# Linear attention beside an MLP: a tile of its own for one head group's rows, sums issued at separate ticks, and a wider pad

## The chip, the cores and the metric

The kernel runs on one core of one Trainium2 chip. The time is device microseconds (us) of that core, the median of several executions. Engines are named as in the profile: PE (TensorE products), PEld (its weight loads), DVE (VectorE), ACT (ScalarE), POOL (GpSimd), SP (SyncE, which issues the DMAs here). `L70` is line 70 of the kernel before.

## The reference

All float32, S = 2048 tokens, D = 640, H = 32 heads of Dh = 20, F = 1728. The result is the input plus an attention branch plus an MLP branch, both on the layer norm of the input:

```
xn  = layernorm(x)
q, k, v = split(xn @ wqkv)                      # per head, 20 wide
pq, pk  = q @ w_phi[h], k @ w_phi[h]
phi     = concat(softmax(p), softmax(-p))       # 40 features per head
o   = phi_q (phi_k^T v) / (phi_q (phi_k^T 1) + 1e-6)
out = x + o @ wo + gelu(layernorm(xn) @ w1 + b1) @ w2 + b2
```

There is no mask: `phi_k^T v` and `phi_k^T 1` are sums over all tokens, so no token's attention output can be made before the last token's `k` and `v`.

## The kernel before

**Numbers.** Each float32 operand is kept as a high and a low part of TensorE's rounded 32-bit type. One product of two operands is three matmuls, high by high, high by low and low by high, which `mm3` issues on lines 70, 71 and 72. Nearly all have 128x128 weights (the stationary operand) and 512 moving columns. In the profile's notation `bank<-y,w` the first name is the moving operand, the second the stationary.

**Stages.** The tokens are four blocks of 512, the hidden units of the MLP 14 chunks of 128 in seven pairs `g`.
- To 215 us: layer norm, transposes, and the MLP for blocks 0 and 1 (`passes`).
- 215 to 446 us: the `q`, `k`, `v` products for 16 tiles of 128 tokens. L895 holds them; each tile takes, over five rows of 128 features, `q` and `k` columns from `wkh` and `wkl`, and the third column group and `v` from tiles named `w`. Their stationary operand is `y`, the normalised tokens. The softmax features of `q` go to DRAM (`e_dram`); those of `k` are multiplied with `v` at once (L965).
- 446 to 478 us: the sums over `k` and `v` become the stationary tiles `kvs`, one for each of 11 head groups.
- 478 to 660 us: the MLP for blocks 2 and 3, with the attention output of all four blocks beside it. For pairs 1 to 5 the method `cross` does w1's part with fewer products, a 2x2 scheme with sums of w1's quarters as weights and sums of the tokens (`tf`) as moving operand; `sums` makes those of w1.
- 660 to 737 us: the product with `wo`, added to the rest and stored.

**What runs beside.** After each triple of products the MLP calls `mlp.tick()`. A tick runs the steps that have come due and moves the generator `beside` one step on. `after(n, step)` puts a step in the list, due in `n` ticks. In the stage from 478 us the order of work on ACT, DVE and POOL is the order in which the program issues it; on each of these engines an instruction that waits holds all behind it. SP's order is chosen by the scheduler.

**Attention's output.** `Attention(b)` takes block `b` through the head groups in the order 10, 0, 1, ..., 9. Groups 0 to 9 have three heads each, group 10 the last two. For a group, `load` brings 128 rows of features from DRAM into `e`, `first` splits them into a high part (ACT, L1195) and a low part (POOL, L1196). Some ticks later `second` issues the products with `kvs` (L1202, L1203) into a bank of PSUM; ACT copies half of the bank's rows into `ts` (L1212), and two ticks later DVE adds the other half (L1216), which frees the bank. For groups 0 to 9 the sum goes to `ob`. For group 10 it goes back into the same rows of `ts`, from which two DMAs send 40 rows of outputs to `o_dram` (L1218) and 2 rows of denominators to `d_dram` (L1219). `ts` is one tile with one buffer.

**Quotients.** Once a block's groups are done, `quotients` gathers the denominators through DRAM into `dt`, takes the reciprocal on DVE (L1235), sends it back, and loads it into five places of `rx` (L1240 to L1245). DVE spreads it over the rows of each head (`stream_shuffle`, L1251) and POOL multiplies the outputs (L1253). This runs beside the next block's groups. L336 and L455 are DVE's own additions and low parts for the MLP; L443, L449 and L452 are ACT's copy, gelu and high part.

**The sums.** `sums(g)` makes one sum and three differences of w1's quarters on POOL in four instructions of 128x256 (L381); ACT and POOL or DVE then split them into the weights of pair `g`. For pairs 2 to 5 it is called by the third of the steps that `gathered` hands to `cross`; for pair 1 before the loop.

**Where tiles lie.** Pools stand on a left and a right side of SBUF. The first pool on the left, `consts`, ends with a tile `pad` that nothing uses (L83). All left tiles of the products (`y`, `m`, `w`, `v`, the accumulators of blocks 0 and 1) begin at a byte of their partition that is 32 modulo 256; the right side's (`wkh`, `wkl`, `tf`, `kvs`, `e`, `ph`) at 224 modulo 256.

Of the kernel before, what the change touches and what calls it, by code (L numbers as in the profile page):

```python
# [8 lines left out]
F32 = mybir.dt.float32  # L9
F32R = mybir.dt.float32r  # L10
AF = mybir.ActivationFunctionType
ALU = mybir.AluOpType
# [3 lines left out]
P = 128  # L16
# [35 lines left out]
def tile_kernel(ctx: ExitStack, tc: tile.TileContext, x, xT, wkT, wqT, wv, wphi, wo, w1, b1, w2, b2,  # L52
                ident, mmask, emask, vsel, out):
    nc = tc.nc
# [20 lines left out]
    cp = ctx.enter_context(tc.tile_pool(name="consts", bufs=1))  # L75
# [4 lines left out]
    mv = cp.tile([P, 16, 2], F32, name="mv")  # L80
    ry = cp.tile([P, 16], F32, name="ry")
    rs_all = cp.tile([P, 16], F32, name="rs_all")
    cp.tile([P, 8], F32, name="pad")  # L83
    nc.vector.memset(ones1, 1.0)
    nc.scalar.activation(rs_all[0:1, 0:1], ones1[:, 0:1], AF.Sqrt)

# [18 lines left out]
    class Banks:  # L105

        def __init__(self, *ids):
            self.ids, self.n = ids, 0
# [15 lines left out]
    def load_x(ts, xp, tag="xb"):  # L124
        xbs = []
        for t in ts:
            xb = xp.tile([P, D], F32, name=tag)
            nc.sync.dma_start(xb, x[t * P:(t + 1) * P, :])
            xbs.append(xb)
        return xbs  # L130
# [83 lines left out]
    class Mlp:  # L214
# [11 lines left out]

        def after(self, ticks, step):

            self.due.append((self.ticks + ticks, len(self.due) and self.due[-1][1] + 1, step))
            self.due.sort(key=lambda d: d[:2])  # L230

        def fetch(self, c, pool=None):

# [94 lines left out]
        def second(self, g, b, w, hid):  # L328

            for m in range(KC):  # L330
                pw = self.po()
                ms = slice(m * P, (m + 1) * P)
                for j, (hh, hl) in enumerate(hid):
                    mm3(pw, w[:, 2 * j, ms], w[:, 2 * j + 1, ms], hh, hl, j == 0, j == 1)
                    self.tick()
                nc.vector.tensor_tensor(acc[b][:, m, :], pw, acc[b][:, m, :], op=ALU.add)  # L336
                yield

        def fetch_pair(self, g, second):

            r1 = rp.tile([P, D], F32, name="r1")
            r2 = rp.tile([P, D], F32, name="r2")
            self.raw[g, second] = r1, r2
            for c, r in ((2 * g, r1), (2 * g + 1, r2)):
                n = min(P, F - c * P)
                if second:
                    for o in range(0, P, n):
                        nc.sync.dma_start(r[o:o + n, :], w2[c * P:c * P + n, :])
                else:
                    nc.sync.dma_start(r.rearrange("p (c f) -> p c f", f=P)[:, :, 0:n], w1[c, :, :, 0:n])  # L350

        def take_pair(self, g, second, slot):

            w = wp.tile([P, 4, D], F32R, name=f"w{slot}")

            def part(j, r):
                hi, lo = w[:, 2 * j], w[:, 2 * j + 1]
                if 0 < g < 6:
                    return self.split(hi, lo, r)
                if 2 * g + j < 13:  # L360
                    split(hi, lo, r, eng=nc.gpsimd)
                elif second:
                    nc.scalar.activation(hi, r, AF.Copy)
                    nc.vector.memset(f(lo[64:128, :]), 0.0)
                    nc.vector.tensor_tensor(lo[0:64, :], r[0:64, :], f(hi[0:64, :]), op=ALU.subtract)
                else:
                    hi, lo, r = (z.rearrange("p (c f) -> p c f", f=P) for z in (hi, lo, r))
                    split(hi[:, :, 0:64], hi[:, :, 64:128], r[:, :, 0:64])
                    nc.vector.memset(f(lo[:, :, 64:128]), 0.0)
                    nc.vector.tensor_copy(lo[:, :, 0:64], f(hi[:, :, 0:64]))  # L370

            return w, [lambda j=j, r=r: part(j, r) for j, r in enumerate(self.raw.pop((g, second)))]

        def sums(self, g):

            raw = [r.rearrange("p (c f) -> p c f", f=P) for r in self.raw[g, False]]
            (a11, a12), (a21, a22) = ((r[:, 0:4:2, :], r[:, 1:4:2, :]) for r in raw)
            s = rp.tile([P, 3, 2, P], F32, name="s")
            for out, x0, x1, op in ((s[:, 0], a21, a22, ALU.add), (a21, a11, a21, ALU.subtract),
                                    (s[:, 1], s[:, 0], a11, ALU.subtract), (s[:, 2], a12, s[:, 1], ALU.subtract)):  # L380
                nc.gpsimd.tensor_tensor(out, x0, x1, op=op)  # L381
            self.raw[g, "s"] = s

        def split(self, hi, lo, src, eng=nc.gpsimd):
# [126 lines left out]
    mlp = Mlp((0, 1, 2, 3), ((0, 2), (1, 3)))  # L511
# [8 lines left out]
    x0 = load_x(range(2), xp)  # L520
    nc.sync.dma_start(idt, ident)
    wc, parts, dmas = {}, {}, {}
# [23 lines left out]
    x1 = load_x(range(4, 8), xp)  # L546
# [16 lines left out]
    def step(gen, n):  # L563
        for _ in range(n):
            next(gen, None)
# [169 lines left out]
    def prep():  # L735
# [60 lines left out]
        for q in range(3):  # L796
            tiles = [(c, b) for c in range(2 * q, min(2 * q + 2, KC)) for b in range(2, 4)]
            for n, at in enumerate(tiles):
                for after, step in ((-6, load), (0, centred), (3, scaled), (5, hi), (7, lo)):
                    events.append((base + 5 * n + after, len(events), step, at))  # L800
            base += 5 * len(tiles) + 5
            if q < 2:
                for n, i in enumerate((0, 2, 1, 3)):
                    for after, step in ((0, combine), (3, lambda q, i: hi(*combined(q, i)[0])), (5, combined_lo)):
                        events.append((base + 4 * n + after, len(events), step, (q, i)))
                base += 19
# [65 lines left out]
    a = ExitStack()  # L872
# [133 lines left out]
    for t, i in [(t, i) for t in range(14) for i in range(4)] + TAIL:  # L1006
# [35 lines left out]
        if (t, i) == (11, 0):  # L1042
            mlp = Mlp((0, 3, 2, 1), ((1, 2), (0, 3)))
            mlp.ph = ptile
            mlp.fetch_pair(0, False)
        if (t, i) == (12, 3):
            with tc.issue_after(evac):
                w1t, parts = mlp.take_pair(0, False, 0)
# [3 lines left out]
        if (t, i) == (15, 3):  # L1052
            w2t, late = mlp.take_pair(0, True, 3)
# [97 lines left out]
    class Attention:  # L1151

        def __init__(self, b, bank):
            self.b, self.n, self.bank = b, 0, bank
            self.ob = acc01.tile([P, KC, 512], F32, name=f"acc{b % 2}")
            self.ts = ep.tile([P, 512], F32, name="ts")
            self.es = {}

        def load(self, g):
# [39 lines left out]
        def second(self, g, ph, pl):  # L1199

            pn = self.bank()
            nc.tensor.matmul(pn, kvs[:, g, :], ph, start=True, stop=False)  # L1202
            nc.tensor.matmul(pn, kvs[:, g, :], pl, start=False, stop=True)  # L1203
            c, h = divmod(g, 2)
            den = d_dram[self.b][0]
            if g < 10:
                a, z = slice(64 * h, 64 * h + VR), slice(64 - 64 * h, 64 - 64 * h + VR)
                t, o = self.ts[a, :], self.ob[a, c, :]
            else:
                a, z = slice(0, 42), slice(64, 106)  # L1210
                t = o = self.ts[a, :]
            nc.scalar.activation(t, pn[z, :], AF.Copy)  # L1212


            def whole():
                nc.vector.tensor_tensor(o, pn[a, :], t, op=ALU.add)  # L1216
                if g == 10:
                    nc.sync.dma_start(o_dram[self.b], o[0:40])  # L1218
                    nc.sync.dma_start(den[30:32, :], o[40:42])  # L1219

            mlp.after(2, whole)
# [78 lines left out]
    ep = rx = None  # L1300
# [42 lines left out]
    ep = ctx.enter_context(tc.tile_pool(name="eB", bufs=1, side="right", reuse_waits="tile"))  # L1343
# [4 lines left out]
    def gathered(g):  # L1348

        w2t, parts = mlp.take_pair(g, True, 0 if g % 2 else 3)  # L1350

        def second():
            parts[1]()
            mlp.after(2, lambda: mlp.fetch_pair(g + 1, False))

        return w2t, [parts[0], second, lambda: g < 5 and mlp.sums(g + 1)]

    for g in range(1, 6):
        w2t, later = gathered(g)
        hid, more = mlp.cross(g, (2, 3), before, later)  # L1360
        if g < 5:
            parts = mlp.splits(g + 1)
        else:
            w1t, parts = mlp.take_pair(6, False, 1)
        for m, _ in enumerate(mlp.second(g, 2, w2t, hid[0])):
            next(more, None)
            if m < len(parts):
                parts[m]()
            if m == 3:
                mlp.fetch_pair(g + 1, True)  # L1370
        before = mlp.second(g, 3, w2t, hid[1])
# [5 lines left out]
    w2t, parts = mlp.take_pair(6, True, 3)  # L1377
# [14 lines left out]
    step = 0  # L1392
# [79 lines left out]
```

## Time and profile before

| | us |
|---|---|
| runs before: median (lowest, highest) | 735.54 (735.34, 735.95) |
| the profiled execution | 739.13 |
| its span, first to last instruction | 737.3 |
| PE busy, 0 to 215 | 215.00 of 215 |
| PE busy, 215 to 446 | 230.67 of 231 |
| PE busy, 446 to 478 | 31.50 of 32 |
| PE busy, 478 to 660 | 168.06 of 182 |
| PE busy, 660 to 737 | 73.92 of 77 |
| mean granted TensorE clock, 478 to 660 | 0.97 |
| mean granted TensorE clock elsewhere | 1.00 |

The rows by stage come from one view that gives each engine's busy time in stretches of the span. Matmuls are pipelined, so a duration in the trace (some 390 ns for 512 columns) is longer than the step from the start of one to the start of the next, and a busy PE can still be made faster by a shorter step. PE is hardly ever idle outside the fourth and the last stretch. Of the fourth, where attention's output runs beside the MLP, it is idle 13.9 us. In the views below, the brackets behind an instruction hold the idle time of its engine just before it, and which engine or DMA ended it.

### The profile page before, as it was taken

The numbers are of one execution on the slowest core, as the hardware profiler recorded it, in microseconds if no ns is written. First come the engines' busy times: TensorE is split into PE (matmuls) and PEld (weight loads), VectorE is DVE, ScalarE is ACT, GpSimd is POOL, SyncE is SP. The second block draws the span as 40 slices with busy tenths as digits, with TensorE's granted clock in tenths as the row PEclk, the third lists the DMA queues.
The fourth block names the chain that finished last, engine by engine and source line by source line (L and its number), as shares of the span: only waits on it lengthen the run. The fifth ranks groups of instructions, "written<-read, shape, count | busy, mean of one in ns | idle before, by whom it ended". The sixth has DMA issues, their size and how long they took to land.

```text
span 737.3 us, 9741 instructions
## 1 busy us (share of the span) xinstructions
PE 713.9 (97%) x3381; PEld 594.6 (81%) x3381; DVE 518.3 (70%) x820; ACT 342.2 (46%) x563; POOL 423.0 (57%) x360
## 2 busy tenths in 40 slices
PE   9989999999999999999999999999989986999998
PEld 7878888878888888888888888888767864878886
DVE  7777756978646887888977896486786853875531
ACT  6534643434235554454445456476665743560110
POOL 3511313675256987887879787585696972641200
PEclk9999999999999999999999999999999998999999
DMA  9813633585531246156005148834354467254122
GB/s 331 281 49 113 195 102 108 170 258 170 196 135 47 70 171 168 55 187 170 1 1 140 43 158 305 239 120 126 114 178 137 135 211 275 66 190 139 72 85 73
DMA packets 65767, 106.56 MB, mean 145 GB/s; under 512 B 7462, under 2 KB 31814, under 8 KB 63838
## 3 DMA queue, kind: packets, MB, share of 16 engines
q1 hardware_dynamic: 65414, 105.93, 44.6%
q8 instruction: 26, 0.43, 0.2%
q14 instruction: 23, 0.19, 0.1%
q10 hardware_dynamic: 304, 0.01, 0.0%
HBM read 71.37 MB, written 34.55 MB: 144 GB/s over the span
## 4 chain that ended last, share of the span: by engine, by line
PE 82%; DVE 5%; POOL 4%; DMA 4%; issue 2%; ACT 2%; SPq 0%; POOLq 0%; ACTq 0%; DVEq 0%
PE bank L895 27%; PE bank L70 15%; PE bank L71 15%; PE bank L72 15%; PE bank L965 2%; PE bank L693 2%; DMA d<-ts 1%; POOL e L1196 1%; POOL w L387 1%; PE bank L1203 1%; PE bank L1202 1%; DMA t<-t 1%; POOL acc L1253 1%; DVE m L455 1%; DMA r<-sr 1%
## 5 line engine op out<-in xcount | busy, mean ns | idle before, releaser
L895 PE MATMUL bank<-wkh,y 128*128 128x512 f32 (+1 forms) x480 | 141.1, 367 | 0.0
L70 PE MATMUL bank<-y,w 128*128 128x512 f32 (+1 forms) x294 | 115.0, 391 | 0.8 <-ACT m L280 0.8
L70 PE MATMUL bank<-m,w 128*128 128x512 f32 x260 | 104.0, 400 | 11.4 <-DVE acc L336 7.1
L72 PE MATMUL bank<-y,w 128*128 128x512 f32 (+1 forms) x294 | 114.3, 389 | 0.0
L71 PE MATMUL bank<-y,w 128*128 128x512 f32 (+1 forms) x294 | 114.2, 389 | 0.0
L64 POOL TENSOR_TENSOR w<-r,w 128x640 fp32r<-128x640 f32 x32 | 53.5, 1684 | 98.8 <-ACT w L61 68.0
L71 PE MATMUL bank<-m,w 128*128 128x512 f32 x260 | 102.2, 393 | 0.0
L72 PE MATMUL bank<-m,w 128*128 128x512 f32 x260 | 102.1, 393 | 0.0
L895 PEld LDWEIGHTS bank<-wkh,y 128*128 128x128 f32 x480 | 87.4, 188 | 14.5
L895 PE MATMUL bank<-wkl,y 128*128 128x512 f32 (+1 forms) x240 | 87.8, 366 | 0.0
L70 PEld LDWEIGHTS bank<-m,w 128*128 128x128 f32 x260 | 49.5, 190 | 24.7 <-DVE acc L336 7.5
L70 PEld LDWEIGHTS bank<-y,w 128*128 128x128 f32 x294 | 55.5, 189 | 12.4 <-ACT m L280 1.0
L72 PEld LDWEIGHTS bank<-y,w 128*128 128x128 f32 x294 | 55.5, 189 | 11.6
L71 PEld LDWEIGHTS bank<-y,w 128*128 128x128 f32 x294 | 55.6, 189 | 11.2
L931 ACT ACTIVATE m<-m,rs_all 128x1280 f32<-128x1280 f32 x32 | 43.7, 1365 | 40.0 <-POOL m L930 39.9
L933 DVE TENSOR_REDUCE sm<-m 128x64 f32<-128x1280 f32 x32 | 47.4, 1480 | 15.4 <-ACT m L931 15.3
L72 PEld LDWEIGHTS bank<-m,w 128*128 128x128 f32 x260 | 49.3, 190 | 10.7
L895 PE MATMUL bank<-w,y 128*128 128x512 f32 x240 | 57.5, 391 | 0.0
L71 PEld LDWEIGHTS bank<-m,w 128*128 128x128 f32 x260 | 49.4, 190 | 10.0
L930 POOL TENSOR_TENSOR m<-m,mx 128x640 f32<-128x640 f32 (+2 forms) x48 | 44.4, 938 | 19.5 <-DVE mx L919 19.5
L325 DVE TENSOR_TENSOR acc<-bank,acc 128x512 f32<-128x512 f32 x70 | 47.0, 683 | 12.0 <-PE bank L321 6.2
L1212 ACT ACTIVATE ts<-bank 64x512 f32<-64x512 f32 (+1 forms) x44 | 26.1, 593 | 56.3 <-PE bank L1203 35.6
(181 smaller groups left out, 1472.1 us busy)
## 6 DMA issues: line engine op xcount, KB each, us to landing
r<-in_w SPq DMA_DIRECT2D x52, 320.0 KB
e<-e SPq DMA_DIRECT2D x40, 256.0 KB
e<-acc SPq DMA_DIRECT2D x52, 160.0 KB
acc<-in_xT SPq DMA_DIRECT2D x4, 1280.0 KB
t<-t SPq DMA_DIRECT2D x8, 512.0 KB
tf<-t SPq DMA_DIRECT2D x2, 1536.0 KB
xb<-in_x SPq DMA_DIRECT2D x8, 320.0 KB
xq<-in_xT SPq DMA_DIRECT2D x10, 256.0 KB
```

The source lines that it names most:

```text
L64: eng.tensor_tensor(lo, src, f(hi), op=ALU.subtract)
L70: nc.tensor.matmul(ps, lh, rh, start=first, stop=False, **kw)
L71: nc.tensor.matmul(ps, lh, rl, start=False, stop=False, **kw)
L72: nc.tensor.matmul(ps, ll, rh, start=False, stop=last, **kw)
L325: nc.vector.tensor_tensor(acc[b][:, m, :], pw, acc[b][:, m, :], op=ALU.add)
L693: nc.tensor.matmul(ps[:, u * nh * DF:(u + 1) * nh * DF], raw[:nh * DH, u * P:(u + 1) * P], wpt[:nh * DH, g, :nh, 1:], start=True, stop=True)
L895: nc.tensor.matmul(ps, lh[:, kc, c], rh[:, kc], start=n == 0, stop=n == 3 * KC - 1)
L930: subs[n, t] = nc.gpsimd.tensor_tensor(ep[:, s], a, b, op=ALU.subtract)
L931: exps[n, t] = nc.scalar.activation(e, e, AF.Exp, scale=rs_all[:, t:t + 1])
L933: nc.vector.tensor_reduce(sm, e.rearrange("p s (h f) -> p (s h) f", f=DH), axis=AX, op=ALU.add)
L965: nc.tensor.matmul(kvp[g // 2][:, (g % 2) * 240:(g % 2) * 240 + 240].rearrange("p (s f) -> p s f", s=4), v[:, g * VS:(g + 1) * VS], ft[:, ...
L1212: nc.scalar.activation(t, pn[z, :], AF.Copy)
```

## The change

Three edits. The tile `pad` gets 56 columns of float32 instead of 8, so that every left tile moves by 192 bytes, from 32 to 224 modulo 256. `sums` takes a number `apart`: its four instructions are issued that many ticks from one another, with the first at once; pairs 2 to 5 pass 1. For this `after` runs a step at once when its ticks are 0. And group 10's rows get a tile `t10` of 42 rows, into which ACT copies, DVE adds and from which the two DMAs read.

```diff
-    cp.tile([P, 8], F32, name="pad")
+    cp.tile([P, 56], F32, name="pad")
...
         def after(self, ticks, step):
 
-            self.due.append((self.ticks + ticks, len(self.due) and self.due[-1][1] + 1, step))
-            self.due.sort(key=lambda d: d[:2])
+            if ticks:
+                self.due.append((self.ticks + ticks, len(self.due) and self.due[-1][1] + 1, step))
+                self.due.sort(key=lambda d: d[:2])
+            else:
+                step()
...
-        def sums(self, g):
+        def sums(self, g, apart=0):
...
-            for out, x0, x1, op in ((s[:, 0], a21, a22, ALU.add), (a21, a11, a21, ALU.subtract),
-                                    (s[:, 1], s[:, 0], a11, ALU.subtract), (s[:, 2], a12, s[:, 1], ALU.subtract)):
-                nc.gpsimd.tensor_tensor(out, x0, x1, op=op)
+            for i, (out, x0, x1, op) in enumerate(((s[:, 0], a21, a22, ALU.add), (a21, a11, a21, ALU.subtract),
+                                                   (s[:, 1], s[:, 0], a11, ALU.subtract), (s[:, 2], a12, s[:, 1], ALU.subtract))):
+                self.after(i * apart, lambda out=out, x0=x0, x1=x1, op=op: nc.gpsimd.tensor_tensor(out, x0, x1, op=op))
...
             self.ts = ep.tile([P, 512], F32, name="ts")
+            self.t10 = ep.tile([42, 512], F32, name="t10")
...
-                t = o = self.ts[a, :]
+                t = o = self.t10[a, :]
...
-        return w2t, [parts[0], second, lambda: g < 5 and mlp.sums(g + 1)]
+        return w2t, [parts[0], second, lambda: g < 5 and mlp.sums(g + 1, 1)]
```

The lines behind the edits move by 3 to 4: L381 becomes L384, L1196 becomes L1200, L1212 becomes L1216. PE, ACT and DVE keep their order; SP's differs by a place in two pairs of neighbours (a weight load beside an `e` load). On POOL the sums are pulled apart. The next rows are POOL's in the fourth stage, at the sums for pair 4; `s` and the tiles `r` belong to the sums, L1196 is the low part of attention's next head group, L1253 the multiplication by the quotients, L387 the first split of a sum. Before:

```order
L1253 TENSOR_TENSOR acc_4392<-acc_4392,rx 128x512
L381 TENSOR_TENSOR s<-r_5013 128x256
L381 TENSOR_TENSOR r_5013<-r_5012,r_5013 128x2x128
L381 TENSOR_TENSOR s<-s,r_5012 128x256
L381 TENSOR_TENSOR s<-r_5012,s 128x256
L1196 TENSOR_TENSOR e<-e,ph 128x512
L1253 TENSOR_TENSOR acc_4392<-acc_4392,rx 128x512
L387 TENSOR_TENSOR w_4358<-r_5012,w_4358 128x640
```

Now:

```order
L1257 TENSOR_TENSOR acc_4392<-acc_4392,rx 128x512
L384 TENSOR_TENSOR s<-r_5015 128x256
L1200 TENSOR_TENSOR e<-e,ph 128x512
L384 TENSOR_TENSOR r_5015<-r_5014,r_5015 128x2x128
L384 TENSOR_TENSOR s<-s,r_5014 128x256
L1257 TENSOR_TENSOR acc_4392<-acc_4392,rx 128x512
L384 TENSOR_TENSOR s<-r_5014,s 128x256
L390 TENSOR_TENSOR w_4358<-r_5014,w_4358 128x640
```

The low part has moved past three of the four sums, and the multiplication past one. At pair 5 it is the same; at pairs 2 and 3 nothing stands between the sums, and the order stays.

On ACT the rows keep their places and only a name changes. These are the ones of block 3, the last: the copy of group 10, two instructions of the MLP, and the copy of group 0. Before:

```order
L1212 ACTIVATE ts<-bank_5618 42x512
L1195 ACTIVATE m_4390<-e 128x512
L449 ACTIVATE m_5488<-m_5488,b1t 128x512
L452 ACTIVATE m_5491<-m_5488 128x512
L1212 ACTIVATE ts<-bank_5646 64x512
L449 ACTIVATE m_5489<-m_5489,b1t 128x512
```

Now:

```order
L1216 ACTIVATE t_5550<-bank_5622 42x512
L1199 ACTIVATE m_4390<-e 128x512
L452 ACTIVATE m_5491<-m_5491,b1t 128x512
L455 ACTIVATE m_5494<-m_5491 128x512
L1216 ACTIVATE ts<-bank_5650 64x512
L452 ACTIVATE m_5492<-m_5492,b1t 128x512
```

The 42-row copy goes to the new tile (`t_5550`), and the 64-row copy of group 0 no longer writes what group 10's DMAs read. The same two rows stand in each of the other blocks.

## The prediction

> **What bounds the kernel now.** I read the page first: the shares of the engines and the chain that ended last.
>
> ```profile
> span 737.3 us, 9741 instructions
> PE 713.9 (97%) x3381; PEld 594.6 (81%) x3381; DVE 518.3 (70%) x820; ACT 342.2 (46%) x563; POOL 423.0 (57%) x360
> ...
> PE 82%; DVE 5%; POOL 4%; DMA 4%; issue 2%; ACT 2%; SPq 0%; POOLq 0%; ACTq 0%; DVEq 0%
> ```
>
> TensorE is the bound nearly everywhere, so time can only come from two places: the step from one product to the next, and the few stalls in between. All that the change reorders or renames lies between 478 and 660 us, where attention's output runs beside the MLP. So next I read the waits of that stretch, and the timeline of PE around each of its long idle times (start, duration, instruction, in brackets the idle time and who ended it).
>
> ```profile
> ACT ts L1212 <- DMA d<-ts: 20.3, 3, 10.4
> ```
>
> ```profile
> 529.28 0.50 PE L1202 MATMUL bank<-m,kvs 128*128 128x512 f32 x1 [0.24 <-DVE acc L1216]
> ...
> 550.52 0.40 PE L1202 MATMUL bank<-ph,kvs 128*128 128x512 f32 x1
> 552.48 0.50 PE L1203 MATMUL bank<-e,kvs 128*128 128x512 f32 x1 [1.56 <-POOL e L1196]
> ...
> 568.31 0.40 PE L1203 MATMUL bank<-e,kvs 128*128 128x512 f32 x1
> 570.50 0.50 PE L70 MATMUL bank<-tf,w 128*128 128x512 f32 x1 [1.79 <-ACT m L443]
> ...
> 593.58 0.50 PE L1202 MATMUL bank<-m,kvs 128*128 128x512 f32 x1 [2.16 <-DVE acc L1216]
> 594.72 0.63 PE L71 MATMUL bank<-y,w 128*128 128x512 f32 x1
> ...
> 616.01 0.39 PE L72 MATMUL bank<-m,w 128*128 128x512 f32 x1
> 623.46 0.80 PE L70 MATMUL bank<-m,w 128*128 128x512 f32 x1 [7.07 <-DVE acc L336]
> 628.23 0.39 PE L70 MATMUL bank<-m,w 128*128 128x512 f32 x1
> ```
>
> Five stalls. Whom PE waits for in three of them is only the last link: behind DVE at 529 and 623 and behind ACT at 570 stands the same wait, ACT's copy into `ts` for head group 0, held until the rows of group 10 have been read out of `ts` by their two DMAs. The chain of waits gives those DMAs' times, the timeline of ACT the longest wait.
>
> ```profile
> 567.08 2.05 DMA d<-ts
> ...
> 612.68 8.72 DMA d<-ts
> ```
>
> ```profile
> 621.50 0.59 ACT L1212 ACTIVATE ts<-bank 64x512 f32<-64x512 f32 x1 [10.41 <-DMA d<-ts]
> ```
>
> The same 4 KB take 2.05 us in one block and 8.72 in the last, since there they queue behind large loads.
>
> **The change part by part.**
>
> *1. A tile of its own for group 10 (L1212, L1216, L1218, L1219).* No instruction is added. ACT's copy for group 0 now waits only for its own products, so all three waits (20.3 us of ACT) go. What PE gets back is less.
> Block 1 (529): 0.24 idle and a slower first product, some 0.5; I take 0.8 with what the late ACT queue costs a little behind it (bounds 0 and 1.2).
> Block 2 (570): 570.50 - 568.31 - 0.23 of a normal step = 1.96, and 0.1 for the slower first product: 2.1.
> Block 3 (623): 623.46 - 616.01 - 0.23 = 7.2, and then the slow clock: from 623.46 to 628.23 there are 11 products in 4.77 us, at 0.227 they would take 2.50, so 2.3 more. Together 9.5, the upper bound. But something else is late next. Block 2's quotients are still on their way: DVE spreads them (`stream_shuffle` on `rx`) in its queue ahead of the additions that free PE's banks, and the five loads of `rx` are issued in the same jam of DMAs.
>
> ```profile
> 621.98 0.51 SPq L1245 DMA_DIRECT2D rx<-d  x1
> ...
> 631.89 0.73 DVE L1251 STREAM_SHUFFLE rx<-rx 128x512 f32<-128x512 f32 x1
> ...
> 633.81 0.69 DVE L1216 TENSOR_TENSOR acc<-bank,ts 64x512 f32<-64x512 f32 x1
> ...
> 636.00 0.39 PE L1202 MATMUL bank<-m,kvs 128*128 128x512 f32 x1
> ```
>
> Today the shuffle comes late enough not to wait. With 9.5 us gone, DVE would come to it at about 622. The last `rx` load, issued at 621.98, lands between 624.0 (2.05 us, as that DMA did in block 2) and 630.7 (8.72, as in the jam); neither row is nearer, and I take the middle, 627.4. So DVE stands from 622 to 627.4 with every addition queued behind it. PE goes on until the pair of products at 636.00 (in the new time 626.5) needs the bank that the L1216 at 633.81 frees. That comes after the shuffle, an L336, an L455 and itself: 627.4 + 0.73 + 0.67 + 0.67 + 0.69 = 630.2. PE thus stands 3.7 us instead of 7.2, at 630.2 instead of 636.0, and pays the slow clock again (2.3), which the 2.16 us stall at 593.58 already draws (0.63 a product behind it, against 0.39). Gain 636.0 - 630.2 - 2.3 = 3.5. Bounds: 0.2 (landing at 630.7) and 9.5 (landing before 622).
>
> *2. The sums of w1, one at a tick (L381).* The same four instructions for POOL; in the two last groups the subtraction for attention's next head group (L1196) now stands behind the first sum instead of behind all four.
>
> ```profile
> 548.15 0.73 POOL L381 TENSOR_TENSOR s<-r 128x256 f32<-128x256 f32 x1
> ...
> 551.16 1.26 POOL L1196 TENSOR_TENSOR e<-e,ph 128x512 fp32r<-128x512 f32 x1
> ```
>
> It starts at 548.9 instead of 551.16 and is done at 550.2, before PE asks at 550.75. The stall at 552.48 goes: 552.48 - 550.52 - 0.23 = 1.73, with its slow first product 1.8. The later sums end about 553.7 instead of 551.2; behind them ACT's and DVE's split of `s` stays where it is, since ACT did not get to it before 553.6 today. So DVE does not move forward with PE here, and after that it waits for a DMA whose chain starts behind the same split:
>
> ```profile
> 562.83 0.95 DVE L1235 RECIPROCAL dt<-dt 128x128 f32<-128x128 f32 x1 [1.59 <-DMA dt<-d]
> ...
> 566.03 0.67 DVE L1216 TENSOR_TENSOR ts<-bank,ts 42x512 f32<-42x512 f32 x1
> ```
>
> The bank that the addition at 566.03 frees is asked for by the pair at 568.08, which would now come at 566.2: 0.5 to 0.8 us of the 1.8 + 2.1 are given back. I take 3.1 for both (bounds 2.1, where the whole 1.8 is lost, and 3.9). The second reordering stands in a stretch where DVE sets the pace (593.58 waits for DVE); the subtraction there must wait for ACT's copy, and the sums behind it with it, for about 1 us of POOL's time under no wait of PE: nothing, bounds -1 and +1.
>
> *3. The pad.* 48 more columns move every tile of the left side by 192 bytes: 32 modulo 256 becomes 224, which `wkh`, `wkl`, `tf`, `kvs`, `e` and `ph` on the right side have already. The trace shows what a step from product to product takes. By the timeline of PE: 15 products with moving `w` (32) on stationary `y` (32) from 308.02, 15 with `wkh`/`wkl` (224) on `y` (32) from 311.46 to 314.96; and 35 in the last stage, all at 32, from 690.05 to 697.98. Behind it, by form, the whole execution, then rows of two stretches (664 to 730 and 478 to 527).
>
> ```profile
> 308.02 3.60 PE L895 MATMUL bank<-w,y 128*128 128x512 f32 x15
> 311.46 0.39 PE L895 MATMUL bank<-wkh,y 128*128 128x512 f32 x1
> ...
> 314.96 1.28 PE L965 MATMUL bank<-w,v 128*128 128x240 f32 x10
> ...
> 690.05 0.39 PE L70 MATMUL bank<-y,w 128*128 128x512 f32 x1
> ...
> 697.98 0.39 PE L72 MATMUL bank<-y,w 128*128 128x512 f32 x1
> ```
>
> ```profile
> L895 PE MATMUL bank<-wkh,y 128*128 128x512 f32 x320 | 105.5, 396 | 0.0
> L895 PE MATMUL bank<-wkl,y 128*128 128x512 f32 x160 | 63.1, 395 | 0.0
> L72 PE MATMUL bank<-tf,w 128*128 128x512 f32 x30 | 11.9, 395 | 0.0
> L71 PE MATMUL bank<-y,w 128*128 128x512 f32 x286 | 112.0, 391 | 0.0
> L71 PE MATMUL bank<-m,w 128*128 128x512 f32 x260 | 102.2, 393 | 0.0
> ...
> L72 PE MATMUL bank<-y,w 128*128 128x512 f32 x76 | 29.6, 389 | 0.0
> ...
> L1202 PE MATMUL bank<-m,kvs 128*128 128x512 f32 x9 | 3.5, 392 | 0.0
> L1202 PE MATMUL bank<-ph,kvs 128*128 128x512 f32 x5 | 2.0, 393 | 0.0
> ```
>
> Steps: 3.44/15 = 229, 3.50/15 = 233, 7.93/35 = 227 ns. Same engines, same stationary `y`: only the moving tile's place differs between 229 and 233. Unlike operands cost 6 ns against 227, and products at 32 that stand between such runs lose 2. If unlikeness is what costs, all go to 227: (320 + 160 + 3 x 30) x 6 = 3.4, and 2 ns on the 240 `w` products between them (15 for each of 16 token tiles), 0.5. The products around attention's groups gain some 0.4 more where DVE doesn't set the pace: 4.3. If it is not, the bounds are the `kvs` rows: both operands at 224 (`ph`) took 393, one (`m`) 392, against 389. No row has a long run with both at 224, which is just what the change makes of everything.
>
> [...] The rows at 229 and 233 don't agree with a step that no address can change, but they don't say which address matters.
>
> **The sum.** 0.8 + 3.1 + 3.5 + 4.3 = 11.7 us off the profiled execution (span 737.3, 739.13 with what lies around it). The unprofiled runs have a median of 735.54; the terms are waits and steps that both have, so 735.54 - 11.7 = 723.8.
>
> **The rivals.**
> [...] Time 735.54 - 7.4 = 728.1.
> *Weights at 224 cost.* The `kvs` rows are the only ones with stationary operands at 224: 3 ns over 389 whatever moves. Then 3 x 286 + 3 x 260 + 240 = 1,878 products get 3 ns more (5.6), the 570 unlike ones 3 less (1.7): 728.1 + 3.9 = 732.0.
> *A moving operand at 224 costs by itself* (slower than before). Every row at 395 has it. Then all 1,878 products step at 233: 1,878 x 6.3 = 11.8, more than the 7.4 from the stalls: 739.9. It decides from 4 ns a product up. Against it: `ph` (393) and `m` (392) should then differ by 6.
> *The quotients don't stand in the way*: `rx` lands by 622, and block 3 gives 9.5 rather than 3.5: 717.8. Against it: its loads are issued at 617 to 622, whatever PE does.
>
> **How the numbers follow.** Forecast (stalls go as worked out, alike operands step at 227): 0.55, its own range 720 to 728. Shift worth nothing 0.18; weights at 224 cost 0.12; moving at 224 costs 0.06; `rx` early 0.09. The range of 717 to 732 takes in the third rival's bounds at its lower end and leaves out the slower case and tails: some 0.8. A measurement here tells 0.2% (1.5 us) from no change. Faster by more than that: all but the slower case and the upper tails, 0.88; within it 0.04; slower 0.08.
>
> **What would show it.** In the changed profile ACT's wait for `d<-ts` is gone from the waits; PE has no idle over 1 us at the places of 550 and 570; a stall of 3 to 5 us stands where DVE waits for DMA `rx<-d` in the last block; and 15 products with `wkh` step in 3.41 us rather than 3.50. It is wrong if the runs at 690 to 698 step slower than 227 ns, if PE's stall in the last block is still 7 us with another name, or if none is left there.

## The result and the profile after

The changed kernel took 724.31 us (median of 4 runs, 722.92 to 726.17) against 735.74 for the kernel before, a ratio of 0.9847 (95% interval 0.9822 to 0.9872): 11.4 us faster, where 11.7 were forecast (723.8). The profiled execution took 725.04, its span 723.1. From profile to profile the gain is thus 14.2, more than between the runs: the profiled execution of before lay 3.4 us above its median, that of after 0.7.

The shares of the page and the waits, in the changed kernel (lines behind the edits are 3 to 4 higher than before: L1200 is the low part of `e`, L1216 ACT's copy, L1220 DVE's addition, L1255 the spread of the quotients, L1206 and L1207 the products with `kvs`):

```profile
span 723.1 us, 9740 instructions
PE 706.7 (98%) x3381; PEld 592.8 (82%) x3381; DVE 513.4 (71%) x820; ACT 341.5 (47%) x563; POOL 421.2 (58%) x360
...
PE 78%; DVE 5%; DMA 4%; POOL 3%; ACT 2%; issue 2%; SPq 0%; DVEq 0%; ACTq 0%; POOLq 0%
```

```profile
DVE rx L1255 <- DMA rx<-d: 5.8, 2, 4.2
```

ACT's wait for `d<-ts`, 20.3 us before, is not among the waits any more. A wait that was not there has come: DVE's for `rx<-d`. PE's timeline shows what became of the five stalls (`[...]` is the idle time before a row):

```profile
545.88 0.39 PE L1206 MATMUL bank<-ph,kvs 128*128 128x512 f32 x1
546.11 0.39 PE L1207 MATMUL bank<-e,kvs 128*128 128x512 f32 x1
...
561.75 0.39 PE L1207 MATMUL bank<-e,kvs 128*128 128x512 f32 x1
561.97 0.39 PE L70 MATMUL bank<-tf,w 128*128 128x512 f32 x1
...
582.76 0.51 PE L1206 MATMUL bank<-m,kvs 128*128 128x512 f32 x1
...
587.31 0.50 PE L1207 MATMUL bank<-e,kvs 128*128 128x512 f32 x1 [1.20 <-POOL e L1200]
...
615.33 0.39 PE L72 MATMUL bank<-y,w 128*128 128x512 f32 x1
619.64 0.80 PE L1206 MATMUL bank<-m,kvs 128*128 128x512 f32 x1 [3.93 <-DVE acc L1220]
620.24 0.63 PE L1207 MATMUL bank<-e,kvs 128*128 128x512 f32 x1
```

The places of 550 and 570 (now 546 and 561.75) go at 0.23 and 0.22 us from product to product, without a stall. That of 593 (now 582.76) has shrunk from 2.16 us to almost nothing, with 1.2 us of another wait behind it. In the last block PE stands 3.93 us instead of 7.07, at another product: the pair that was to be reached at 636 before.

Both timelines hold the same 3,381 products in the same order, so the lead of the changed kernel can be read at any of them: start before less start after. Lead gained in each stretch (places by the time in the kernel before), with the same for four of the experiments below:

| stretch (us) | forecast | changed | t10 alone | sums alone | pad alone | t10 and sums |
|---|---|---|---|---|---|---|
| 0 to 528 | 3.4 | 3.2 | 0.1 | 0.0 | 3.6 | -0.5 |
| 528 to 545 (block 1) | 0.8 | 1.4 | 1.2 | 0.1 | 0.1 | 1.2 |
| 545 to 556 (stall at 552) | 1.8 | 1.9 | 1.3 | 1.8 | -2.5 | 1.8 |
| 556 to 580 (stall at 570) | 1.3 | 2.3 | 2.0 | -3.1 | 2.1 | 2.0 |
| 580 to 605 (stall at 593) | 0 | 1.9 | -0.5 | 1.8 | 0.4 | 1.9 |
| 605 to 670 (stall at 623) | 3.5 | 3.6 | 2.1 | 0.5 | 1.9 | 6.9 |
| sum | 11.7 | 14.3 | 6.1 | 1.1 | 5.6 | 13.2 |

(Of the pad's 4.3 in the forecast, 3.4 belong to the first row; 0.9 for `tf` and the products around attention's groups lie in several stretches and stand in the sum alone. What was to be given back, 0.8 at most, is taken off at 570.) These are single executions, and every sum contains the 3.4 us by which the profiled execution of before lay above its median. The pad's -2.5 at 552 is a stall that grew from 1.56 to 2.47 us in that execution, with slow clock behind it (0.61 us for the first product, where it took 0.50 before). The last row moves most from one execution to the next: it is 3.6 and 3.3 in two of the changed kernel and 6.7 in `e6_right_at_32` below, whose order of work is the same. The verdicts on the experiments therefore rest on the runs.

### The profile page after: what moved, and what is told of

It reads as the page before. It is cut to its first block, busy times and chain, and to the rows that moved or that the text cites. A ratio compares the mean times of both kernels' runs of the same rounds, so it can differ in the third digit from the quotient of the medians.

```text
span 723.1 us, 9740 instructions
## 1 busy us (share of the span) xinstructions
PE 706.7 (98%) x3381; PEld 592.8 (82%) x3381; DVE 513.4 (71%) x820; ACT 341.5 (47%) x563; POOL 421.2 (58%) x360
## 4 chain that ended last, share of the span: by engine, by line
PE 78%; DVE 5%; DMA 4%; POOL 3%; ACT 2%; issue 2%; SPq 0%; DVEq 0%; ACTq 0%; POOLq 0%
PE bank L898 23%; PE bank L70 16%; PE bank L72 15%; PE bank L71 15%; PE bank L968 2%; PE bank L696 2%; POOL m L933 2%; DMA tf<-ob 1%; PE bank L1207 1%; PE bank L1206 1%; DMA rx<-d 1%; POOL m L944 1%; DMA t<-t 1%; DVE sm L936 1%; ACT w L61 1%
## 5 line engine op out<-in xcount | busy, mean ns | idle before, releaser
L898 PE MATMUL bank<-wkh,y 128*128 128x512 f32 (+1 forms) x480 | 139.5, 364 | 0.0
L898 PEld LDWEIGHTS bank<-wkh,y 128*128 128x128 f32 x480 | 87.5, 188 | 13.2
L70 PEld LDWEIGHTS bank<-m,w 128*128 128x128 f32 x260 | 48.9, 188 | 16.7 <-DVE acc L328 6.0
L72 PEld LDWEIGHTS bank<-m,w 128*128 128x128 f32 x260 | 48.8, 188 | 10.3
L71 PEld LDWEIGHTS bank<-m,w 128*128 128x128 f32 x260 | 48.9, 188 | 9.6
L898 PEld LDWEIGHTS bank<-w,y 128*128 128x128 f32 x240 | 44.4, 188 | 8.5
```

Source lines behind the costliest of these rows:

```text
L70: nc.tensor.matmul(ps, lh, rh, start=first, stop=False, **kw)
L71: nc.tensor.matmul(ps, lh, rl, start=False, stop=False, **kw)
L72: nc.tensor.matmul(ps, ll, rh, start=False, stop=last, **kw)
L898: nc.tensor.matmul(ps, lh[:, kc, c], rh[:, kc], start=n == 0, stop=n == 3 * KC - 1)
```

## The experiments

### One part alone, and two

`e1_t10` is the changed kernel with the pad at 8 columns and the sums all at once; `e2_sums` has only the sums apart, `e3_pad` only the pad, `e4_t10_sums` all but the pad.

```diff
# e1, e2, e4
-    cp.tile([P, 56], F32, name="pad")
+    cp.tile([P, 8], F32, name="pad")
# e1, e3
-        return w2t, [parts[0], second, lambda: g < 5 and mlp.sums(g + 1, 1)]
+        return w2t, [parts[0], second, lambda: g < 5 and mlp.sums(g + 1)]
# e2, e3
-            self.t10 = ep.tile([42, 512], F32, name="t10")
...
-                t = o = self.t10[a, :]
+                t = o = self.ts[a, :]
```

> The tile of its own for group 10 alone, on the kernel before. By the prediction's terms 0.8 + 2.1 + 3.5 = 6.4 us: 729.3, with the 2.16 us stall of PE in block 2's later groups (593.58 in the kernel before) still there. Rival: that stall was ACT's late copy too, passed on through DVE's queue; then it is gone here (under 0.5 us) and the time is about 727.3. In both, ACT's wait for the DMA d<-ts is gone, the 1.6 us stall for POOL's e stays, and DVE waits 2 to 7 us for the DMA rx<-d in the last block.

> The sums of w1 one at a tick, alone, on the kernel before. By the prediction's terms 1.8 less the 0.5 to 1.8 given back behind it: 734.2 to 735.7, with the stalls of 1.8 us (ACT's copy) and 7 us (DVE) in blocks 2 and 3 still there. Rival: the 2.16 us stall at 593.58 belongs to the sums for pair 5; then it goes here and the time is 732 or less.

> The pad of 56 columns alone, on the kernel before: no wait is removed. By the prediction 4.3 us: 731.4. By the changed kernel's trace, where PE had gained 2.3 us in L895 and 3.1 us by 510 us, some 3 to 3.5 us: 732.4. If the shift is worth nothing: 735.7. Products with moving wkh or wkl step at 227 ns instead of 233, those with stationary kvs at 227 instead of 229.

> The changed kernel with the old pad of 8 columns. If the terms add: the changed kernel's 724.3 plus 3.1 to 4.3 for the pad: 727.4 to 728.6; 735.7 - 0.8 - 3.1 - 3.5 = 728.3 by the prediction's own terms. If the stalls that went in the changed kernel needed the shorter steps as well (PE reaching a place at another moment), the time is over 729.5 and a stall of more than 1 us stands between 560 and 600 us.

Measured, beside 737.84 for the kernel before on that chip: t10 alone 730.36, ratio 0.9901 (0.9871 to 0.9932), 7.3 us; sums alone 736.85, 0.9994 (0.9976 to 1.0012), no change that can be told; pad alone 735.38, 0.9963 (0.9944 to 0.9983), 2.7 us; t10 and sums 727.48, 0.9867 (0.9841 to 0.9893), 9.8 us. The three alone make 10.4 together, the change 11.4. What `e4_t10_sums` asked is answered too: without the pad no stall of more than 1.2 us stands between 560 and 600 us, so the stalls that went did not need the shorter steps.

**The sums alone** are worth nothing, though their stall goes. PE comes 1.8 us earlier to the next place, and waits there longer for ACT, which still stands until group 10's rows have left `ts`. The waits, and PE's timeline in block 2 of `e2_sums`:

```profile
ACT ts L1216 <- DMA d<-ts: 10.0, 2, 5.7
```

```profile
566.82 0.40 PE L1207 MATMUL bank<-e,kvs 128*128 128x512 f32 x1
570.16 0.50 PE L70 MATMUL bank<-tf,w 128*128 128x512 f32 x1 [2.94 <-ACT m L446]
...
592.75 0.50 PE L1206 MATMUL bank<-m,kvs 128*128 128x512 f32 x1
...
597.32 0.50 PE L1207 MATMUL bank<-e,kvs 128*128 128x512 f32 x1 [1.19 <-POOL e L1200]
```

2.94 us instead of 1.79, and 1.8 of slow clock behind it: more than the 1.8 is given back. The two edits need each other there. And the row at 592.75 is the place of the 2.16 us stall, which is gone here, while `e1_t10` still has it:

```profile
589.59 0.51 PE L1206 MATMUL bank<-m,kvs 128*128 128x512 f32 x1 [2.69 <-DVE acc L1220]
```

In these two profiles it goes with the sums for pair 5 and not with ACT's copy (what lies behind that comes below): the rival in `e2_sums` was right on the place, and wrong on the whole time, since it left out what block 2 gives back.

**t10 alone** gave 7.3 us. The interval, 5.0 to 9.5, holds both the forecast's terms (6.4) and the rival (8.4); the stall at 589.59 above, which the rival had gone, is what refutes it. In the last block DVE waits for the quotients there too, longer than in the changed kernel:

```profile
DVE rx L1255 <- DMA rx<-d: 8.4, 2, 5.8
```

### Which addresses cost

`e6_right_at_32` puts the left side back to 32 and the right side there too; `e7_left_at_96` and `e8_left_at_160` change the left pad alone.

```diff
# e6 (e7: 24 columns, e8: 40, without the two pads on the right)
-    cp.tile([P, 56], F32, name="pad")
+    cp.tile([P, 8], F32, name="pad")
...
     wkv_ = [kvw.tile([P, KC, CN], F32R, name=f"wk{p}") for p in "hl"]
+    kvw.tile([P, 48], F32, name="padw")
...
     bp = ctx.enter_context(tc.tile_pool(name="bconst", bufs=1, side="right", reuse_waits="tile"))
+    accp.tile([P, 48], F32, name="padr")
```

> The changed kernel with the left side back at 32 modulo 256 and the right side (wkh, wkl, tf, kvs, e, ph) moved to 32 as well by a pad of 48 columns there. If it is likeness that counts: all products step at 227 ns, with wkh and wkl too, as in the changed kernel, 724 to 725. If it is that nothing on the left may lie at 32, or a right operand at 224 that is slow by itself: in the first case y on w steps over 230; in the second all is at 227 too, which this run can't tell from likeness, but the changed kernel (wkh at 224, 227 ns) has ruled it out already.

> The changed kernel with a pad of 24 columns: the left side at 96, the right at 224, so unlike modulo 256 but alike modulo 128. If modulo 256 counts: wkh and wkl on y and tf on w step at 233 ns, kvs at 229, and 3 to 4 us more than the changed kernel. If modulo 128 or less counts: 227 ns.

> The changed kernel with a pad of 40 columns: the left side at 160, the right at 224, alike modulo 64 alone. If modulo 256 or 128 counts: 233 ns for wkh, wkl and tf; if modulo 64 counts: 227 ns. A cost that grows with the distance would be lower here than with 96 and 32.

`e6_right_at_32`: 723.1 us (2 runs), ratio 0.9825 (0.977 to 0.9879), like the changed kernel. `e7_left_at_96` took 729.70 and `e8_left_at_160` 732.91, one run each, beside 735.39 for the kernel before: the steps below tell more than these times, since `e8_left_at_160` also has a stall of 2.74 us that comes below. By form, of the changed kernel, of `e6_right_at_32` and of `e8_left_at_160` (last come busy time and mean ns; before: 396 for `wkh`, 393 for `ph`):

```profile
L898 PE MATMUL bank<-wkh,y 128*128 128x512 f32 x320 | 104.0, 392 | 0.0
...
L1206 PE MATMUL bank<-ph,kvs 128*128 128x512 f32 x16 | 6.2, 389 | 0.0
```

```profile
L899 PE MATMUL bank<-wkh,y 128*128 128x512 f32 x320 | 104.0, 392 | 0.0
...
L1208 PE MATMUL bank<-ph,kvs 128*128 128x512 f32 x16 | 6.2, 389 | 0.0
```

```profile
L898 PE MATMUL bank<-wkh,y 128*128 128x512 f32 x320 | 105.0, 395 | 0.0
...
L1206 PE MATMUL bank<-ph,kvs 128*128 128x512 f32 x16 | 6.5, 406 | 0.0
```

In these rows, alike at 224 and alike at 32 are the same to the nanosecond. At 160 against 224 (and at 96 against 224, where `wkh` on `y` has 396 again) the products pay. From start to start, the median from `wkh` to `wkh` on `y` is 233 ns before (32 against 224), 237 at 96, 229 at 160, and 227 where both are alike; from `m` to `e` on `kvs` 229, 241, 236 and 227 (226 in the changed kernel). So it is likeness that counts here, neither 32 nor 224 is bad by itself, and operands that were 64 or 128 bytes apart modulo 256 were not alike enough. The products around one count as well as its own two operands: from `ph` to `e` on `kvs` all lies at 224 in the kernel before too, yet the step was 229 ns there, 231 in `e7_left_at_96` and 229 in `e8_left_at_160`, and 227 only where the whole kernel is alike (medians of 15 steps). The order of the costs differs between `wkh` and `kvs`; what sets their size stays open.

That rules out the three other cases for the pad: that it is worth nothing (728.1), that weights at 224 cost, and that a moving operand at 224 costs by itself. A product's step was not free of where its operands lie: 233 ns against 227 for `wkh` on `y`.

The gain was less than forecast, 2.45 us over the `q`, `k`, `v` products instead of 3.4: 2.34 of the 2.9 for `wkh` and `wkl`, and 0.11 of the 0.5 for the `w` products between them. The timeline of the changed kernel shows why: 15 products with `wkh` and `wkl` took 3.40 us from 310.03 to 313.43, 227 ns each as forecast, but only every second such group does so.

```profile
310.03 0.39 PE L898 MATMUL bank<-wkh,y 128*128 128x512 f32 x1
...
313.43 0.84 PE L968 MATMUL bank<-w,v 128*128 128x240 f32 x6
```

The groups right behind the products of `k`'s features with `v` (L968) take 233 ns a product (235.6 before), in `e6_right_at_32` too. The forecast took one group for all. In the changed kernel these others run in: from the first product to the second 270 ns, and 226 to 227 from the twelfth on (medians of 12 groups). What makes them run in was not tried. Addresses are not ruled out: `v`, which the section ahead of the prediction puts with the other left tiles, begins in the built programs at 160 modulo 256 before and at 96 after the change, so nearly all products of L968 have unlike operands in every kernel here.

### The stall that was left

In the changed kernel SP issues the last `rx` load at 609.79, DVE stands from 612.06 to 616.23 at the first spread, and frees the bank for PE's pair only with the addition at 618.89:

```profile
609.79 0.51 SPq L1249 DMA_DIRECT2D rx<-d  x1
```

```profile
611.39 0.67 DVE L339 TENSOR_TENSOR acc<-bank,acc 128x512 f32<-128x512 f32 x1
616.23 0.01 DVE L1255 LOAD_MASK_SELECT rx<-rx  x1 [4.17 <-DMA rx<-d]
...
618.89 0.69 DVE L1220 TENSOR_TENSOR acc<-bank,ts 64x512 f32<-64x512 f32 x1
```

Three kernels move that wait; the changed kernel ran again beside the last two.

```diff
# e5, e9: 16 ticks; e10: 14
-            for i in range(6):
+            for i in range(16 if self.b == 2 else 6):
                 yield
             for c in range(KC + 1):
...
# e10
-                for i in range(3):
+                for i in range(1 if self.b == 2 else 3):
...
# e9, e10: first_split()
+        for c in range(5):
+            yield
         for c in range(KC + 1):
             at[0].split(c, nc.vector)
-            if c % 2:
-                yield
+            yield
```

> The changed kernel, with block 2's five spreads of the quotients (and POOL's multiplications behind them) issued ten ticks later, some 6.8 us. If the stall left in the last block is DVE standing at the first spread for the DMA rx<-d (4.17 us there, 4.1 us lost by PE, 1.4 us of slow clock behind it), all of it goes: 5.5 us faster than the changed kernel, 718.8, and no wait of DVE for rx<-d over 1 us. Rival: the later spreads only move the wait to block 3's quotients or to the start of the last stage; then under 2 us, 722.3 or more, and a new stall of several us stands behind 640.

`e5_late_shuffle`: 723.5 us, 0.9825 (0.9794 to 0.9856), not to be told from the changed kernel; the rival was right, though its stall came at 636.7 to 640.6 and not behind 640. The stall went (5.7 us of lead at that place), DVE no longer waits for `rx<-d`, and 4.1 us came back at 636, where DVE had the five splits of L1278 (the first at 630.70) and two late spreads ahead of the addition that frees a bank. PE, then DVE:

```profile
640.62 0.60 PE L70 MATMUL bank<-m,w 128*128 128x512 f32 x1 [3.93 <-DVE acc L328]
```

```profile
633.63 3.56 DVE L1278 TENSOR_TENSOR y<-tf,y 128x512 fp32r<-128x512 f32 x4
...
637.96 0.72 DVE L1255 STREAM_SHUFFLE rx<-rx 128x512 f32<-128x512 f32 x1
...
639.89 1.27 DVE L328 TENSOR_TENSOR acc<-bank,acc 128x512 f32<-128x512 f32 x2
```

> The changed kernel once more, beside the two below on one chip: ratio 0.983 to 0.987 to the kernel before, PE losing 2.4 to 4.5 us in the last block while DVE waits for rx<-d.

> As e5_late_shuffle (block 2's spreads ten ticks later), and the split of block 0's attention output for the last stage (DVE L1278) starts five ticks later, one column group a tick instead of two. If the 4.1 us that PE lost at 636 in e5_late_shuffle are DVE's queue of those five splits and the last two spreads ahead of L328's additions, this loss goes and the time is 4 to 5.5 us under the changed kernel: 718 to 720. If the loss came from elsewhere (the weights' DMA, ACT), a stall of 3 us or more stays there and the time is that of e5_late_shuffle, 723.

> As e9_late_both, but block 2's spreads start eight ticks later instead of ten and follow each other at one tick instead of three, so all are done before the splits. The same 4 to 5.5 us under the changed kernel if DVE's queue has room for five spreads in six ticks (0.65 us each); a stall of 1 to 2 us of PE at 620 to 626 if it has not, and then 720 to 721.

Beside a kernel before of 737.41: the changed kernel 725.91, 0.984 (0.9821 to 0.9859); `e9_late_both` 719.22, 0.975 (0.9733 to 0.9767), the fastest, 6.7 us under the changed kernel where 4 to 5.5 were expected; `e10_late_close` 723.99, 0.9813 (0.9796 to 0.983). The profile of `e9_late_both` has two short stalls left at that place:

```profile
638.72 0.50 PE L70 MATMUL bank<-m,w 128*128 128x512 f32 x1 [1.06 <-DVE acc L328]
...
640.50 0.47 PE L70 MATMUL bank<-m,w 128*128 128x512 f32 x1 [0.36 <-DVE acc L328]
```

`e10_late_close` missed both of its theories. DVE had room for five close spreads, but each spread sets free a multiplication on POOL, and four of them stood ahead of the low part that PE needed. POOL, then PE:

```profile
625.20 5.03 POOL L1257 TENSOR_TENSOR acc<-acc,rx 128x512 f32<-128x512 f32 x4
630.17 1.86 POOL L1200 TENSOR_TENSOR e<-e,ph 128x512 fp32r<-128x512 f32 x1
```

```profile
632.09 0.50 PE L1207 MATMUL bank<-e,kvs 128*128 128x512 f32 x1 [3.14 <-POOL e L1200]
```

### Why the stall at 593 went

From 564 to 580 us `e1_t10` and `e4_t10_sums` run alike, DVE and ACT within 0.1 us; POOL's order differs, by the sums for pair 5. Then one kind of row parts them, DVE's low parts (L458), which read two tiles of SBUF as POOL's instructions do. `e1_t10`, POOL and DVE:

```profile
580.38 1.30 POOL L1257 TENSOR_TENSOR acc<-acc,rx 128x512 f32<-128x512 f32 x1
581.63 2.04 POOL L390 TENSOR_TENSOR w<-r,w 128x640 fp32r<-128x640 f32 x1
```

```profile
580.45 1.78 DVE L458 TENSOR_TENSOR m<-m,m 128x512 fp32r<-128x512 f32 x1
```

`e4_t10_sums`, POOL and DVE:

```profile
580.59 1.76 POOL L1257 TENSOR_TENSOR acc<-acc,rx 128x512 f32<-128x512 f32 x1
```

```profile
580.52 0.68 DVE L458 TENSOR_TENSOR m<-m,m 128x512 fp32r<-128x512 f32 x1
```

Where POOL started 0.07 us ahead, DVE took 1.78 us: POOL's end at 581.63 and the usual 0.6 behind it. Where DVE started 0.07 us ahead, it took 0.68, and POOL's instruction 1.76 instead of 1.30. Two such low parts in a row, 1.1 and 1.2 us late, are the stall of `e1_t10`; in the kernel before the second alone took that long (the first 1.23 us):

```profile
591.00 1.93 DVE L455 TENSOR_TENSOR m<-m,m 128x512 fp32r<-128x512 f32 x1
```

`e7_left_at_96` and `e8_left_at_160` differ only in their pads and both have t10 and the sums apart; DVE's low part took 0.68 and 1.89 us there, and only `e8_left_at_160` has the stall, 2.74 us. Its rows, DVE and POOL, start 0.01 us apart, too close to tell which was first:

```profile
579.36 1.89 DVE L458 TENSOR_TENSOR m<-m,m 128x512 fp32r<-128x512 f32 x1
```

```profile
579.37 1.33 POOL L1257 TENSOR_TENSOR acc<-acc,rx 128x512 f32<-128x512 f32 x1
```

In `e7_left_at_96` POOL started 0.05 us behind DVE; the sums, which wait for a DMA, began 0.17 us earlier relative to PE in `e8_left_at_160`. In the 14 profiles of this case the stall stands where at least one of the two low parts ahead of it took 1.8 us or more, and in no other. It stands in all four profiles with the sums at once and in one of the ten with the sums apart: the sums' place goes with it nearly always, but `e8_left_at_160` shows that it doesn't remove it by itself. That the order of arrival decides is what the rows say; no experiment here set that order.

One experiment was to set it with work added:

```diff
# on e1; idle: a tile of 128x192 that nothing reads
             self.raw[g, "s"] = s
+            if g == 5:
+                nc.gpsimd.memset(idle[:, 0:160], 0.0)
```

> e1_t10 (the tile for group 10 alone) with work added: one POOL memset of 128x160 of a tile that nothing reads, some 0.24 us, behind the four sums of pair 5. In e1_t10 DVE's low parts (L458) at 580.45 and 587.05 start 0.07 to 0.2 us behind a POOL instruction and take 1.78 and 1.90 us; in e4_t10_sums they start 0.07 to 0.1 us ahead of one and take 0.68. If it is this order of arrival that makes PE's stall at 586.51 (2.86 us and 1.8 of slow clock) and not the place of the sums, both low parts take about 0.7 us here, the stall is under 0.6 us and the slow clock behind it is gone, and PE leaves 605 us some 2.4 us earlier than in e1_t10, although work was added. Rival: the sums have to be apart, so that the split of ph (L1200) comes ahead of them: then the stall stays at 2.7 to 3.1 us. The whole time, with the stall in the last block changing from run to run, 727 to 730.

It was inconclusive: 730.06 us, 0.9917 (0.9887 to 0.9947), and the stall stayed, 2.73 us. The memset took its 0.24 us, but the sums, which wait for a DMA, began 0.24 us earlier relative to PE than in `e1_t10`, and POOL was ahead of DVE by 0.06 us again:

```profile
579.91 1.31 POOL L1259 TENSOR_TENSOR acc<-acc,rx 128x512 f32<-128x512 f32 x1
```

```profile
579.97 1.81 DVE L460 TENSOR_TENSOR m<-m,m 128x512 fp32r<-128x512 f32 x1
```

Both rows are as the order of arrival has it; the order itself was not changed, so the rival is not refuted by this run. `e8_left_at_160` shows that sums apart are not enough; that they are not needed stays unshown, since no profile here has the sums at once and no stall.

## Why the prediction was right

**The time** was: 11.4 us of 11.7. The four signs that were named came: ACT's wait for `d<-ts` gone, nothing over 1 us at the places of 550 and 570, a stall of 3 to 5 us where DVE waits for `rx<-d`, and 15 products with `wkh` in 3.40 us. The steps were right in kind, several sizes were not, and that the time met the forecast is in part luck. The sum was worked out from the profiled execution, and from profile to profile the gain was 14.3: 2.6 more than forecast (570 gave 1.0 too much, 593 1.9 and block 1 0.6, the pad's terms less than forecast). The runs gained less than the profiles, since the profiled execution of before was slower than its median by 3.4 us.

**A tile for group 10.** All three waits of ACT went. Block 1 gave 1.4 for the 0.8 forecast, above its bound of 1.2 (1.2 with the tile alone). Block 2's 1.79 us stall went whole. In the last block the new wait came where it was put: DVE at the spread, 4.17 us for the DMA `rx<-d`, with the pair that was at 636 held up. PE lost 4.1 us for the 3.7 forecast; the slow clock behind it cost 1.6 instead of 2.3; the gain was 3.6 for 3.5. `e5_late_shuffle` and `e9_late_both` show that it was this wait: without it that place gains 5.7 us more in both. The spread had been put to wait from 622 to 627.4, 5.4 us; it waited 4.2. Two errors stand behind that: the spread was set free 6.4 us behind the issue of the last `rx` load instead of 5.4, and DVE came to it 2.3 us behind that issue instead of with it. In the eight profiles with the tile and the spreads in their old place, the first time is 6.1 to 6.9 us, the second 1.0 to 4.3, and the gain of that row 2.1 to 6.9; so 3.6 for 3.5 is luck too, from a landing that the prediction put in the middle of its bounds for want of a nearer row.

**The sums.** The stall at 552 went as worked out (1.8 of lead). The step on what is given back failed: "So DVE does not move forward with PE here". It did, since ACT came to the split of `s` 5.3 us earlier (553.62 before, 548.37 after), and the chain behind it followed: DVE's reciprocal was 5.6 us earlier (562.83 and 557.25) where PE was 6.5 ahead. Nothing of the 0.5 to 0.8 was given back. With the sums alone everything is, by another wait, ACT's.

**The second reordering**, "nothing, bounds -1 and +1", gave 1.9. The stall at 593 was read as DVE's pace, and the row that holds it (a low part of 1.93 us where the same form took 0.68 elsewhere) was not looked at. The cause, as far as the rows show it, is the order of arrival above; the trace of before shows that order for its own kernel and not for the changed one.

**The pad.** Unlike operands did cost 6 ns and alike ones stepped at 227 (`wkh` on `y`); that likeness is the cause is shown by `e6_right_at_32`. Mis-sized was the count: 4.3 forecast, 3.2 and 3.6 up to 528 us in the profiles of the changed kernel and of the pad alone, 2.7 (1.3 to 4.1) in the runs of the pad alone. No run shows a shift worth nothing (728.1, the forecast without the 4.3; chance 0.18). Two steps of the sum failed. Half the groups with `wkh` and `wkl` run in behind L968 and took 233 ns on average instead of 227. And "products at 32 that stand between such runs lose 2" does not hold: the 15 `w` products of a group took 229 ns each before and 228 after, since they too run in, over the first eight in the kernel before and the first five in the changed one.

## What to carry to other kernels

Before a wait is removed, look for the next thing on the queue of the engine that is set free, and price it by when that thing's data lands: here a DMA took back 4 us that a later place in the queue, with room made behind it, gave again (719.2 instead of 725.9). Edits around one bottleneck need not add: the sums alone were worth nothing that can be told, and with the tile some 2.5 us (9.8 less 7.3). With intervals of some 2 us on each, the runs leave that difference open; the traces show the 1.8 us given back in one case and kept in the other. Where a step from product to product differs by a few nanoseconds between groups of like shape (here 233 and 227), compare the operands' addresses modulo 256, and look at more than one group: here every second one ran in behind products of another shape.

## What was not expected of the hardware

- Of two instructions of DVE and POOL that both read SBUF, the one that started 0.07 us behind ended late, DVE by 1.1 us (1.78 for 0.68, `e1_t10`) or POOL by 0.46 (1.76 for 1.30, `e4_t10_sums`).
- PE's clock after a stall (all stalls over 1 us behind 400 us, in the 14 profiles): by the idle time in brackets, no stall up to 1.8 us was followed by products at 427 ns instead of 227, and every one of 2.47 us or more was, at a cost of 1.6 to 3.0 us. Of the four between, 2.02 (`e3_pad`) and 2.16 us (the kernel before) were and 2.23 and 2.36 (`e4_t10_sums`) were not: a longer stall left the clock alone where a shorter one did not, and no run shows what decides it. In the changed kernel the granted clock was 0.71 from 620 to 625 us, behind its 3.93 us, and 1.00 from 625 to 630.
